# B over 128 array lines: real and imaginary part of one frequency in one output of M

## The chip, the cores and the metric

The kernel runs on one core of a Trainium2 chip. The metric is the device time of one execution in microseconds (us). The engines are called as in the profile: PE is TensorE (PEld its weight loads), ACT is ScalarE, DVE is VectorE, POOL is GpSimd, and SP only issues DMAs. Each engine works through its own instructions in the order in which the program issues them.

## The reference

Eight sequences of 3008 rows with 256 channels go through a Fourier layer and then a two-layer perceptron:

```python
X = np.fft.rfft(x, axis=1)                       # per batch, over the 3008 rows
Yr = Xr @ w_r - Xi @ w_i + b_r
Yi = Xr @ w_i + Xi @ w_r + b_i
Y  = soft_threshold(Yr, 0.01) + 1j * soft_threshold(Yi, 0.01)
y  = np.fft.irfft(Y, n=3008, axis=1)
h  = y @ w_in                                    # 256 -> 2048
g  = where(h > 0, h, exp(min(h, 0)) - 1)
out = g @ w_out                                  # 2048 -> 256
```

## The kernel before

3008 is 47 x 64, and each transform is made of two short ones. Per batch five kinds of unit follow one another:

- **A**, six units: a matmul with the 64-point matrix `M1` over 8 columns of x, copied to SBUF and stored to DRAM (`DA`).
- **X**, eight units: `Z` is read back from `DA` in another order, and eight matmuls of 96 rows against `M2` make the spectrum. A copy (`evac`, on ACT in the main part) puts it into `XT`, channels in partitions, a real plane and an imaginary plane, for 24 values of `k` times 64 values of `n2`.
- **M**, twelve units (six `q` with `i` = 0 and 1): four matmuls of 128x512. The weights of PE are 128 columns of `XT` (two `k` times 64 `n2`), the moving operand is `wcat_r` = [w_r, w_i] against the real plane and `wcat_s` = [-w_i, w_r] against the imaginary one. Output partitions are 128 frequencies, output columns are 256 real and 256 imaginary channels. DVE adds the bias (`yb`), POOL clips and subtracts, giving `Y`.
- **B**, six units: the inverse 64-point step. A frequency's real and imaginary part lie in different columns of `Y`, and each `k` owns 64 partitions, so a unit is eight matmuls over 64 partitions each, in pairs on the two halves of the array (`s` = 0, 1), two accumulated for each output. ACT copies the two PSUM banks to `Bz`, and `Bz` goes to DRAM (`DB`).
- **Y**, eight units: `Bs` is read back from `DB`, matmuls with `M4` give `yT`.

The perceptron runs in 376 iterations of 512 rows by 256 of the 2048 inner channels, 47 to a batch. An iteration has a `front` (four matmuls into `hps`, then ELU on ACT, DVE or POOL into `gT`) and the `back` of the iteration two before (eight matmuls into `ps_o`). `plan` puts at most one unit of the next batches ahead of each front, in the order X0 to X7, then M, M, B and so on, then A and Y. All units of the main part share one PSUM buffer (`psF`, one buffer), so that the copy out of a unit must be over before the next unit's first matmul. `hps` has two buffers.

The first batch has no perceptron to lie beside. It runs ahead of the loop: tables are computed on POOL, DVE and ACT (`points`, `phases`, `wraps`, `signs`, `sizes`, `sines`; group 0 to 3 of `M2`), then A, X with two PSUM buffers (copies of X1, X4 and X7 on DVE, the others on ACT), M (`first_M`, half of them with the bias added by a matmul and the clipping on ACT and DVE) and B, with short runs of idle matmuls (`idle_pe`) between. In this stretch the tables of `M3` for B are made: `v3` at L559, `w3` at L599 and L600, its absolute value at L606 after X1, two sines at L613 after X7, two multiplications at L617 and L621 beside the first M. `gate` makes POOL wait for `Z`, and behind it POOL issues the three loads of x for batch 1 and half of `w_out`, ahead of all X units.

## Time and profile before

| | |
|---|---|
| median of 3 runs | 912.52 us (912.39 to 912.84) |
| the profiled execution | 911.36 us, of which its span is 909.6 us |
| PE busy | 893.2 us, 98% of the span |
| DVE, ACT, POOL busy | 717.5, 696.8, 314.9 us |
| M (L192), matmuls 128x512 | 384, of them 48 ahead of the loop |
| B (L244), matmuls 64 rows x 256 | 384, of them 48 ahead of the loop |
| first front | 56.5 us after the span's start |

A line of the timeline or of the chain gives the start in us from the span's start, the duration, the engine, the line of the kernel and the tiles (output, arrow, inputs). Several instructions of one kind are merged ("x8"), and then the duration is from the start of the first to the end of the last. The chain of work that ended last gives only the share that nothing else covered. Matmuls overlap: a 128x512 matmul lasts 0.38 us and the next starts 0.216 us behind it.

### The profile page before, as it was taken

The numbers are of one execution on the slowest core, as the hardware profiler recorded it, in microseconds if no ns is written. First come the engines' busy times: TensorE is split into PE (matmuls) and PEld (weight loads), VectorE is DVE, ScalarE is ACT, GpSimd is POOL, SyncE is SP. The second block draws the span as 40 slices with busy tenths as digits, with TensorE's granted clock in tenths as the row PEclk, the third lists the DMA queues.
The fourth block names the chain that finished last, engine by engine and source line by source line (L and its number), as shares of the span: only waits on it lengthen the run. The fifth ranks groups of instructions, "written<-read, shape, count | busy, mean of one in ns | idle before, by whom it ended". The sixth has DMA issues, their size and how long they took to land.

```text
span 909.6 us, 17270 instructions
## 1 busy us (share of the span) xinstructions
PE 893.2 (98%) x6721; PEld 652.3 (72%) x6721; DVE 717.5 (79%) x891; ACT 696.8 (77%) x850; POOL 314.9 (35%) x438
## 2 busy tenths in 40 slices
PE   8989999999999999999999999999999999999997
PEld 3447667876688667886678766787667866777775
DVE  8669778887788778897788877888778877778776
ACT  6768788777878778787787888778887877767664
POOL 6701540333321441405404153033332134443664
PEclk9999999999999999999999999999999999999999
DMA  8997116721283215732166032752228111231011
GB/s 270 309 269 228 47 48 186 209 70 47 77 241 124 71 47 143 190 109 85 56 201 194 24 99 59 217 161 72 69 72 230 30 42 47 82 82 48 24 48 46
DMA packets 90670, 106.24 MB, mean 117 GB/s; under 512 B 5270, under 2 KB 81308, under 8 KB 87228
## 3 DMA queue, kind: packets, MB, share of 16 engines
q1 hardware_dynamic: 84332, 77.62, 30.6%
q0 software_dynamic: 5968, 27.26, 9.1%
q8 instruction: 52, 0.85, 0.4%
q10 hardware_dynamic: 288, 0.26, 0.1%
q14 instruction: 30, 0.25, 0.1%
HBM read 55.32 MB, written 49.81 MB: 116 GB/s over the span
## 4 chain that ended last, share of the span: by engine, by line
PE 85%; DVE 5%; ACT 3%; DMA 3%; issue 2%; POOL 1%; SPq 1%; DVEq 0%; ACTq 0%; POOLq 0%
PE ps_o L773 34%; PE hps L715 34%; PE mps L192 9%; PE yps L282 2%; PE bps L244 2%; PE xps L175 2%; PE aps L144 2%; DMA Bs<-DB 2%; DVE gT L742 1%; DVE Et L754 1%; ACT Et L729 1%; ACT Et L726 1%; DMA xt<-in_x_dram 1%; DVE osb L784 1%; ACT Bz L257 1%
## 5 line engine op out<-in xcount | busy, mean ns | idle before, releaser
L773 PE MATMUL ps_o<-w_out_r,gT 128*128 128x256 f32 x3008 | 477.0, 301 | 0.2 <-DVE gT L740 0.2
L773 PEld LDWEIGHTS ps_o<-w_out_r,gT 128*128 128x128 f32 x3008 | 403.4, 189 | 50.3 <-DVE osb L784 1.3
L715 PE MATMUL hps<-yT,w_in_s 128*128 128x512 bf16 (+4 forms) x1728 | 389.9, 353 | 2.5 <-DVE gT L742 1.2
L740 DVE SCALAR_TENSOR_TENSOR gT<-Et,hps 128x512 fp32r<-128x512 f32 (+1 forms) x272 | 222.8, 848 | 75.3 <-POOL Et L752 38.2
L742 DVE SCALAR_TENSOR_TENSOR gT<-hps,Et 128x1024 fp32r<-128x1024 f32 x198 | 242.2, 1223 | 16.5 <-PE ps_o L773 1.0
L715 PEld LDWEIGHTS <-w_in_s 128*128 128x128 bf16 x1728 | 141.6, 98 | 129.4 <-issue 23.0
L729 ACT ACTIVATE Et<-hps 128x1024 f32<-128x1024 f32 x198 | 204.0, 1030 | 13.2 <-PE hps L715 6.7
L752 POOL TENSOR_SCALAR Et<-Et 128x512 f32<-128x512 f32 x187 | 111.4, 615 | 222.9 <-ACT Et L724 222.9
L754 DVE TENSOR_SCALAR Et<-Et 128x1024 f32<-128x1024 f32 x198 | 137.0, 692 | 48.0 <-ACT Et L729 40.1
L210 POOL TENSOR_SCALAR clip<-yb 128x512 f32<-128x512 f32 x84 | 51.7, 615 | 316.0 <-DVE yb L202 278.6
L724 ACT ACTIVATE Et<-hps 128x512 f32<-128x512 f32 x188 | 102.1, 595 | 63.9 <-PE hps L715 63.9
L726 ACT ACTIVATE Et<-hps 128x1024 f32<-128x1024 f32 x84 | 86.3, 1027 | 71.5 <-PE hps L715 71.0
L211 POOL TENSOR_TENSOR Y<-yb,clip 128x512 bf16<-128x512 f32 x84 | 107.2, 1276 | 7.0
L727 ACT ACTIVATE Et<-Et 128x1024 f32<-128x1024 f32 x84 | 88.8, 1058 | 2.7
L202 DVE TENSOR_TENSOR yb<-mps,bias_bc 128x512 f32<-128x512 f32 x89 | 61.4, 689 | 35.4 <-PE mps L192 28.6
L127 ACT CAST XT<-xps 128x768 bf16<-128x768 f32 x61 | 48.8, 800 | 15.8 <-PE xps L175 15.8
L127 ACT CAST yT<-yps 128x752 bf16<-128x752 f32 x63 | 49.7, 788 | 14.2 <-PE yps L282 14.1
L192 PE MATMUL mps<-wcat_r,XT 128*128 128x512 bf16 x192 | 58.2, 384 | 0.8 <-ACT Bz L257 0.3
L127 ACT CAST A<-aps 128x1024 bf16<-128x1024 f32 x45 | 45.6, 1014 | 15.3 <-PE aps L144 13.8
L192 PE MATMUL mps<-wcat_s,XT 128*128 128x512 bf16 x192 | 57.1, 379 | 0.0
L192 PEld LDWEIGHTS <-XT 128*128 128x128 bf16 x384 | 30.8, 98 | 29.6 <-DVE XT L125 0.6
L257 ACT CAST Bz<-bps 128x1024 bf16<-128x1024 f32 x46 | 46.0, 1000 | 2.5 <-PE bps L244 2.5
(110 smaller groups left out, 412.9 us busy)
## 6 DMA issues: line engine op xcount, KB each, us to landing
xt<-in_x_dram POOLq DMA_DIRECT2D x21, 1024.0 KB, 7.1
out_dram<-osb SPq DMA_DIRECT2D x158, 128.0 KB
Bs<-DB SPq DMA_DIRECT2D x32, 384.0 KB
DA<-A SPq DMA_DIRECT2D x21, 512.0 KB
DB<-Bz SPq DMA_DIRECT2D x21, 512.0 KB
Z<-DA SPq DMA_DIRECT2D x7, 1152.0 KB
Z<-DA SPq DMA_DIRECT2D x11, 384.0 KB
xt<-in_x_dram POOLq DMA_DIRECT2D x6, 512.0 KB, 5.9
```

What stands on the lines that cost most here:

```text
L127: nc.scalar.copy(dst, src)
L192: nc.tensor.matmul(ps, lhsT=XT[:, dt, c, o : o + P], rhs=wm[:, dt, :], start=(not biased and m == 0 and dt == 0), stop=(m == 1 and dt == 1),)
L211: nc.gpsimd.tensor_tensor(Y_of[b, q][:, i, :], yb, clip[:], ALU.subtract)
L715: nc.tensor.matmul(hps[:, s, c0:c1], lhsT=w_in_s[:, dt, ft * P : ft * P + P], rhs=yT_of[b][:, dt, t0 : t0 + c1 - c0], start=(dt == 0), sto ...
L724: nc.scalar.activation(E_[:, s], hps[:, s], AF.Exp)
L726: nc.scalar.activation(E_, hps[:], AF.Relu, scale=-1.0)
L729: nc.scalar.activation(E_, hps[:], AF.Exp)
L740: nc.vector.scalar_tensor_tensor(o, e, -1.0, h, ALU.add, ALU.max)
L742: nc.vector.scalar_tensor_tensor(o, h, 0.0, e, ALU.max, ALU.add)
L752: eng.tensor_scalar(E_[:, s], E_[:, s], 1.0, 0.0, ALU.min, ALU.max)
L754: nc.vector.tensor_scalar(E_, E_, 1.0, -1.0, ALU.min, ALU.add)
L773: nc.tensor.matmul(po[q][:, i_ % 2, :], lhsT=gT[:, s, i_ * P : i_ * P + P], rhs=w_out_r[:, ft, :], start=(ft == 0 and i_ % 2 == 0), stop=( ...
```

## The change

- `XT` has for each `k` three runs of 64: minus imaginary, real, imaginary. `M2`'s columns are put in that order, ACT (or DVE) copies real and imaginary part, and a new POOL instruction behind each copy writes minus imaginary (128 x 384 elements), 64 in all.
- An M group takes one `k` at a time. Its weights are the 128 columns [real, imaginary] against w_r and [minus imaginary, real] against w_i, so that real and imaginary part of one frequency are 128 output partitions and 256 columns hold the channels. That is eight matmuls of 128x256 in place of four of 128x512. `wcat_s` goes, and the bias becomes a column of 128 values by 256.
- A B unit is four matmuls over all 128 partitions, none accumulated, in place of eight over 64. The two PSUM banks hold `i` = 0 and 1. Where the copy is split between ACT and DVE, each takes one bank.
- `M3` has real and imaginary rows in its two halves of partitions. It is built in two helper tiles `T3` and put in place by four DMAs from SP. The work for `T3` (`v3`, `w3`, its absolute value, two sines) moves ahead of `wraps(3)`, that is ahead of half of `M2`'s sines; the two multiplications move behind X1's copy, and the pieces of the bias from behind X1 to behind X4.
- POOL's loads of x for batch 1 move from ahead of X to behind X1, X3 and X7, and that of `w_out` to behind the first M.

```diff
             k = 8 * g + kk
             nc.tensor.matmul(
                 psv[:, kk, 0 : 4 * K1], lhsT=Z[:, k, dt * P : dt * P + P],
-                rhs=M2[:, k].rearrange("p c m -> p (c m)"), start=True, stop=True,
-            )
-        xv = XT[:, dt].rearrange("p c (m s) -> p c m s", s=NS)[:, :, :, 8 * g : 8 * g + 8]
-        pv = psv[:, :, 0 : 4 * K1].rearrange("p k (c m) -> p c m k", c=2)
-        evac(xv, pv, on_dve)
+                rhs=M2[:, k].rearrange("p k c t -> p (k c t)"), start=True, stop=True,
+            )
+        xv = XT[:, dt].rearrange("p k (a s) -> p k a s", s=NS)[:, :, :, 8 * g : 8 * g + 8]
+        pv = psv[:, :, 0 : 4 * K1].rearrange("p j (k a) -> p k a j", a=4)
+        evac(xv[:, :, 2:6], pv, on_dve)
+        nc.gpsimd.tensor_scalar(xv[:, :, 0:2], xv[:, :, 4:6], -1.0, None, ALU.mult)
...
     def m_group(b, q, i, ps, biased=False):
         XT = XT_of[b]
-        o = (2 * q + i) * P
-        if biased:
-            nc.tensor.matmul(ps, lhsT=busy[:, 0:P], rhs=bias_p[:], start=True, stop=False)
-        for m, (c, wm) in enumerate(((0, wcat_r), (1, wcat_s))):
-            for dt in range(2):
+        for e in range(2):
+            k, pe = 4 * q + 2 * i + e, ps[:, e * D : e * D + D]
+            if biased:
                 nc.tensor.matmul(
-                    ps, lhsT=XT[:, dt, c, o : o + P], rhs=wm[:, dt, :],
-                    start=(not biased and m == 0 and dt == 0), stop=(m == 1 and dt == 1),
+                    pe, lhsT=bias_p[:, D : D + P], rhs=bias_p[:, 0:D], start=True, stop=False
                 )
+            for c in range(2):
+                for dt in range(2):
+                    nc.tensor.matmul(
+                        pe, lhsT=XT[:, dt, k, (1 - c) * N2 : (1 - c) * N2 + P],
+                        rhs=wcat_r[:, dt, c * D : c * D + D],
+                        start=(not biased and c == 0 and dt == 0), stop=(c == 1 and dt == 1),
+                    )
...
-            nc.vector.tensor_tensor(yb, ps, bias_bc[:], ALU.add)
+            nc.vector.tensor_tensor(
+                yb.rearrange("p (e d) -> p e d", e=2), ps.rearrange("p (e d) -> p e d", e=2),
+                bias_bc[:].unsqueeze(1).to_broadcast([P, 2, D]), ALU.add,
+            )
...
-        for pp in range(2):
-            for c in range(2):
-                for s in range(2):
-                    nc.tensor.matmul(
-                        ps[:, s, pp * D : pp * D + D],
-                        lhsT=M3[s * N2 : s * N2 + N2, 2 * v + pp, c, :],
-                        rhs=Y[s * N2 : s * N2 + N2, pp, c * D : c * D + D],
-                        start=(c == 0), stop=(c == 1),
-                    )
+        for i in range(2):
+            for e in range(2):
+                nc.tensor.matmul(
+                    ps[:, i, e * D : e * D + D], lhsT=M3[:, e, 2 * v + i, :],
+                    rhs=Y[:, i, e * D : e * D + D], start=True, stop=True,
+                )
         o = 4 * (v % 2)
-        Bv = Bz[:, o : o + 4, :].rearrange("p (q s) d -> p s q d", s=2)
-        psv = ps[:].rearrange("p s (q d) -> p s q d", d=D)
+        Bv = Bz[:, o : o + 4, :].rearrange("p (i e) d -> p i (e d)", i=2)
         if on_dve:
-            nc.scalar.copy(Bv[:, :, 0], psv[:, :, 0])
-            nc.vector.tensor_copy(Bv[:, :, 1], psv[:, :, 1])
+            nc.scalar.copy(Bv[:, 0], ps[:, 0])
+            nc.vector.tensor_copy(Bv[:, 1], ps[:, 1])
         else:
-            nc.scalar.copy(Bv, psv)
+            nc.scalar.copy(Bv, ps[:])
...
-        pool.tensor_scalar(wcat_s[:, :, 0:D], w_i_f[:], -1.0, None, ALU.mult)
-        pool.tensor_copy(wcat_s[:, :, D : 2 * D], w_r_f[:])
         for g in range(4):
...
+            pool.tensor_scalar(
+                bias_p[:, D + N2 * c : D + N2 * c + N2], busy[:, 0:N2], (c0, c1)[c][:], None,
+                ALU.mult,
             )
...
         sines(1, 1)
+        slot0()
+        full = [P, NV, N2]
+        dve.scalar_tensor_tensor(
+            v3[:], n2row.unsqueeze(1).to_broadcast(full), 1.0 / S,
+            k3[:].unsqueeze(2).to_broadcast(full), ALU.mult, ALU.mult,
+        )
+        dve.tensor_scalar(w3[:], v3[:], CMAGIC, -CMAGIC, ALU.add, ALU.add)
+        dve.tensor_tensor(w3[:], v3[:], w3[:], ALU.subtract)
+        nc.scalar.activation(a3[:], w3[:], AF.Abs)
+        T3 = [wk4.tile([P, NV, P], BF16, name="T3", tag="Bs") for _ in range(2)]
+        for o, src, sc, bi in ((1, w3, TURN, 0.0), (0, a3, -TURN, hpi[:])):
+            nc.scalar.activation(
+                T3[0][:, :, o * N2 : o * N2 + N2], src[:], AF.Sin, bias=bi, scale=sc
+            )
         wraps(3)
         signs(2)
-        slot0()
         sines(2, 0)
         sizes(3)
         sines(2, 1)
...
     load_w_in(0)
-    gate(Z_of[0][:, 8, 0:1])
-    for ci in range(3):
-        load_x(1, ci)
-    load_w_out(0)
...
         unit_X(0, u, alone=True, on_dve=u in (1, 4, 7))
         if u == 1:
-            nc.scalar.activation(a3[:], w3[:], AF.Abs)
-            nc.vector.tensor_copy(bias_p[32:64], rest[32:64])
-            nc.vector.tensor_copy(bias_p[64:P], rest[64:P])
-            nc.vector.tensor_tensor(rest[64:P], rest[64:P], bias_p[64:P], ALU.subtract)
-            nc.vector.tensor_copy(bias_p[64:P], rest[64:P])
+            for o in range(2):
+                nc.vector.scalar_tensor_tensor(
+                    T3[1][:, :, o * N2 : o * N2 + N2], T3[0][:, :, (1 - o) * N2 : (2 - o) * N2],
+                    2.0 - 4.0 * o, sgb, ALU.mult, ALU.mult,
+                )
+            for c in range(2):
+                for e in range(2):
+                    nc.sync.dma_start(
+                        M3[N2 * c : N2 * c + N2, e], T3[c][N2 * e : N2 * e + N2]
+                    )
+        if u == 4:
+            nc.vector.tensor_copy(bp[32:64], rest[32:64])
+            nc.vector.tensor_copy(bp[64:P], rest[64:P])
+            nc.vector.tensor_tensor(rest[64:P], rest[64:P], bp[64:P], ALU.subtract)
+            nc.vector.tensor_copy(bp[64:P], rest[64:P])
+        if u == 1:
+            gate(Z_of[0][:, 8, 0:1])
+            load_x(1, 0)
+        if u in (3, 7):
+            load_x(1, (u - 1) // 2 - u // 7)
         idle_pe(1)
-    for o, src, sc, bi in ((1, w3, TURN, 0.0), (0, a3, -TURN, hpi[:])):
-        nc.scalar.activation(
-            M3[:, :, 0, o * N2 : o * N2 + N2], src[:], AF.Sin, bias=bi, scale=sc
-        )
-    sgb = sg3[:].unsqueeze(2).to_broadcast([P, K1 // 2, N2])
-    nc.vector.scalar_tensor_tensor(
-        M3[:, :, 1, 0:N2], M3[:, :, 0, N2:P], 2.0, sgb, ALU.mult, ALU.mult
-    )
     first_M(0, 0, False)
-    nc.vector.scalar_tensor_tensor(
-        M3[:, :, 1, N2:P], M3[:, :, 0, 0:N2], -2.0, sgb, ALU.mult, ALU.mult
-    )
+    load_w_out(0)
```

## The prediction

> **What bounds the kernel now.** I read the page's shares and chain first, then the chain around one B unit, then the timeline there engine by engine, then the opening (the first 57 us), and last the busy time and clock by stretch.
>
> ```profile
> PE 893.2 (98%) x6721; PEld 652.3 (72%) x6721; DVE 717.5 (79%) x891; ACT 696.8 (77%) x850; POOL 314.9 (35%) x438
> ```
>
> PE is the bound nearly everywhere, so a change on PE counts in full where nothing else is late next. The chain of work around unit B0 of batch 1 (start, duration):
>
> ```profile
> 99.25 0.86 PE hps L715 x4
> 100.11 0.92 PE ps_o L773 x8
> 101.03 0.54 PE bps L244 x8
> 101.57 0.97 PE hps L715 x4
> 102.54 0.92 PE ps_o L773 x8
> ```
>
> Only PE stands in it. B costs 0.54, and the front behind it 0.97 where its neighbour costs 0.86: 0.65 us in all. But in the timeline ACT is close behind:
>
> ```profile
> 100.15 1.03 ACT L726 ACTIVATE Et<-hps 128x1024 f32<-128x1024 f32 x1
> 101.20 1.06 ACT L727 ACTIVATE Et<-Et 128x1024 f32<-128x1024 f32 x1
> 102.17 0.99 ACT L257 CAST Bz<-bps 128x1024 bf16<-128x1024 f32 x1
> 103.31 0.39 PE L192 MATMUL mps<-wcat_r,XT 128*128 128x512 bf16 x1
> ```
>
> Three ACT instructions run back to back from the front of the M iteration, and the copy of B (ends 103.16) frees the one PSUM buffer 0.15 before the next M starts.
>
> The opening matters because it runs once with nothing beside it. Its lines, columns as before, idle time before in brackets:
>
> ```profile
> 23.81 0.80 ACT L127 CAST XT<-xps 128x768 bf16<-128x768 f32 x1 [2.10 <-PE xps L175]
> 24.61 0.94 DVE L125 CAST XT<-xps 128x768 bf16<-128x768 f32 x1
> ...
> 31.97 0.95 DVE L621 SCALAR_TENSOR_TENSOR M<-M,sg 128x768 bf16<-128x768 bf16 x1
> 32.15 1.24 POOL L230 TENSOR_SCALAR clip<-yb 128x512 f32<-128x512 f32 x1 [3.16 <-DVE yb L202]
> ...
> 46.85 0.59 ACT L254 CAST A<-bps 128x512 bf16<-128x512 f32 x1 [0.31 <-PE bps L244]
> 47.47 0.69 DVE L255 CAST A<-bps 128x512 bf16<-128x512 f32 x1 [1.10 <-ACT A L254]
> ```
>
> ACT has 2.1 us to spare before X0's copy, and none after. POOL's clip takes 1.24 beside DVE's L621, 0.61 elsewhere. B5's two half copies run one after the other. And by stretch (PE busy, PEld, DVE, ACT, POOL, clock):
>
> ```profile
> 23.30:30.50 7.20, 5.71 (x74) 3.53 (x74) 6.24 (x10) 5.46 (x8) 5.49 (x7) 1.00 0.93 251
> 30.50:46.80 16.30, 16.30 (x106) 6.99 (x106) 9.79 (x14) 11.68 (x16) 10.83 (x12) 1.00 1.03 326
> 54.00:57.40 3.40, 1.74 (x20) 1.03 (x20) 1.26 (x2) 0.79 (x1) 0.00 (x0) 1.00 1.04 318
> 57.40:60.90 3.50, 3.50 (x23) 2.04 (x21) 1.61 (x2) 2.14 (x3) 1.47 (x2) 0.51 1.03 271
> ```
>
> From 30.5 to 46.8 PE never pauses; after 3.4 us in which PE was half busy, the clock was 0.51 for the next 3.4.
>
> **The change, part by part.**
>
> *B, in the loop.* Four matmuls of 128x256 replace eight on half arrays. Full-array bf16 matmuls of that width exist:
>
> ```profile
> 485.46 1.05 PE L715 MATMUL hps<-yT,w_in_s 128*128 128x256 bf16 x8
> ```
>
> Eight last 1.05 with 0.27 for the last one, so 0.11 each, with a weight load under every one. A B unit becomes 4 x 0.11 = 0.44 and saves 0.21; 42 units in the loop could give 8.8. Next late is ACT's copy. Where PE does wait for it (copy over at 214.19, next unit at 214.24) the gap is 0.05. I read the gap for B0 to B3 of the seven batches: 24 of 28 show 0.14 to 0.19, four show 0.05. Gap less 0.05, summed, is 2.7. Behind B5 the front comes 0.10 after gT of two iterations before, which hangs on the same ACT row; so B4 and B5 together give 0.05 in six batches and some 0.3 in the last, where no A unit follows: 0.6. Total -3.3. The new copy runs through its banks in order, as A's does (1014 ns for 128x1024 at L127, against 1000 at L257): 28 x 0.014 = +0.4.
>
> *M.* 8 x 0.109 to 0.111 replaces 4 x 0.216: 0 to 0.02 more for each of 96 groups; start by start the steps of such rows are 0.109 and 0.216, so I take 0.005: +0.5 (bounds 0 and +1.9). DVE's addition (689 ns) keeps its elements.
>
> *Negation in the loop, 56 of them.* The nearest rows are the clip, 615 ns for 512 elements, so 0.46 for 384, and a cast of 128x512 to bf16 at 604; I take 0.50, with 0.46 and 1.24 as ends. In the X iterations POOL is idle, and ACT's copy of X7 ends at 89.38 with M's first matmul at 90.18. The negation ends by 89.95, and the first matmul to read it is M's third, at 90.4: cost 0, and if it took 1.24, some 0.3 in each of seven batches, +2. ACT's copy has the same 768 elements, and ACT rows go by elements (752 in 788 ns, 768 in 800): 0.
>
> *The opening: tables.* On DVE v3 (0.95), w3 (0.85 and 1.25) and slot0 (0.66) now stand ahead of wraps(3), so w3 is there at 18.1 + 3.7 = 21.8, where ACT waits for it from 18.7. Behind it on ACT: absolute value 0.85, sines 0.85 and 0.92, then five table instructions at some 0.45 and the bias copy at 0.3. X0's copy starts at 26.5, 2.7 late; the 2.1 us of cover is gone. DVE: X1's copy 27.0 to 27.95, the two multiplications (0.95 each) to 29.85, X4's copy to 30.8, the bias pieces (halved, 1.2) to 32.0, X7's copy to 32.95, against 30.44 before: +2.5.
>
> *The opening: POOL's queue.* Eight negations, the gate (0.4) and two loads (0.65 each) pass through POOL ahead of M. The negation of X1 meets the two multiplications, and by the row at 32.15 it gets through only behind them, at about 30.3. Then gate, load, two negations, load and four more: 0.4 + 1.3 + 6 x 0.5 = 4.7, so X7's is done at 35.0, and M's matmuls on minus imaginary wait for it. The second M group starts at 35.6 instead of 31.15: +4.5 (bounds: +2.5 if POOL keeps pace, +7 with negations of 0.9). The third load and that of w_out stand behind; B1 needs POOL's second Y some 6.4 us after that start and gets it at 5.9. The x loads have until A at 46.75, now some 50: 0. wcat_s no longer costs POOL 2.20 and 0.60, and two one-column products (nearest row 536 ns) come in; POOL was done with it at 25.59, ahead of the first negation: 0. SP gets four DMAs for M3, two of which wait for the multiplications; nothing is queued behind them before B0's store, and B0 is 8 us away: 0 (a store of 256 KB, DB<-A, lands in 2.8).
>
> *The opening: clock.* PE has 3 us without work behind X1 and another 2 before M. By the rows at 54.0 and 57.4 a stretch half empty is followed by 3.4 us at 0.51, in which M loses up to 1.7, over two stretches 3.4; the X stretch before, 5.71 busy of 7.20, kept 1.00. Between 0 and 3.4 I take the middle: +1.7. The Trainium skill ("TensorE: Matmul & The Clock Gate", Part 1: The HAM clock gate) lets the clock fall only after an idle window of about 3.4 us; by that rule the term would be 0 and the sum 0.65. The trace does not agree: the window ahead of the 0.51 held 1.74 us of matmuls.
>
> *The opening: B.* B0 to B3 lie on PE: 4 x 0.21 = -0.8. B4 and B5 wait for the last Y instead (45.68 + 0.69, and B5's second half behind it): 0. B5's two half copies each read half of both banks, and DVE began 0.02 after ACT ended; at 79.33 and 79.41 DVE and ACT copy two tiles of ps_o at once. With a bank each, DVE starts 0.62 earlier: -0.65 (bounds -0.65 and 0).
>
> **Sum.** -3.3 + 0.4 + 0.5 + 0 + 4.5 + 1.7 - 0.8 - 0.65 = +2.35 us. The profiled execution took 911.36 us (span 909.6), 1.16 below the median of 912.52; the sum makes it 913.7, and 912.52 + 2.3 = **914.8** on the median's scale. A difference of 0.2%, 1.8 us, is about what a measurement of this kernel can tell from none.
>
> **The rivals.**
>
> 1. *The opening absorbs the tables (not slower).* If POOL keeps pace with the copies, M starts 2.5 late and the clock stays at 1.00. For it: POOL has less to do in this stretch without wcat_s, and 23.3 to 30.5 kept its clock. Against it: the row of 1.24. The sum is zero where M's delay and the clock's term together are 3.85. Here it is 2.35 - 2.0 - 1.7 = -1.35, so 911.2; a little more of B's saving brings it below 910.7.
> 2. *B's saving arrives whole (faster).* If the copy is not late, the loop gives -8.8 in place of -2.9, and the sum is -3.6: 908.9. Against it stand the three ACT rows; it needs Bz to start 0.1 earlier, and nothing in the change makes L726 or L727 shorter.
> 3. *Negations are slow.* At 1.1 us the opening loses another 6 x 0.6 = 3.6, and in the loop a negation that starts at 89.43 ends at 90.53, past the start of DVE's next SBUF-to-SBUF instruction (L754, 90.51), which could be held as the clip was by L621. The front two iterations on has 0.10 to spare for that, and each 0.02 past it costs 56 x 0.02 = 1.1. Sum about +7: 919.5.
> 4. *The change doesn't shorten B.* If the step stayed at 0.65, the loop and the opening gain nothing: 2.35 + 2.9 + 0.8 = +6, so 918.5. The 0.11 rows speak against it.
>
> **How the numbers follow.** Forecast 0.48 (own range 913.2 to 917: two thirds, 0.32, slower by over 1.8, the rest, 0.16, within); rival 1 0.21 (0.14 within, 0.07 faster); rival 2 0.13 (faster); rivals 3 and 4 0.13 and 0.05 (slower). Faster 0.20, within 0.30, slower 0.50. The range leaves out most of rival 2 and the far half of rival 3: **909.8 to 919.5**.
>
> **What would show it.** X0's copy on ACT near 26.5; POOL without a pause from X1's negation to X7's; the second M group near 35.6; a clock below 1.00 between 27 and 41; B5's halves side by side. In the loop: B and the front behind it in 0.44 + 0.86, the next unit 0.05 behind the copy, M at 0.88, X7's negation over before M starts. The forecast is wrong if M starts by 33.5, if PE's gaps behind Bz stay at 0.15 with B shorter, or if negations last 0.8 or more.

## The result, and the profile after

The changed kernel takes **923.97 us** (median of 4 runs, 922.86 to 924.65) against 912.52 before. The ratio is 1.0119, 95% interval 1.0103 to 1.0135. The sign of the forecast held; its size did not: 914.8 was forecast, and the time lies 4.5 us above the range. The profiled execution took 922.86 us (span 920.8), 11.50 more than that of before.

The page of the changed kernel, the shares of the engines:

```profile
PE 889.6 (97%) x6818; PEld 698.7 (76%) x6920; DVE 717.1 (78%) x891; ACT 695.7 (76%) x850; POOL 386.9 (42%) x502
```

PE has 3.6 us less to do than before, and the kernel is 11.5 longer: PE waits more. POOL has 72 us more, nearly all of it in one group. The groups of POOL by form (line, engine, operation, tiles, shapes, count, then busy time, mean ns of one, idle time before):

```profile
L181 POOL TENSOR_SCALAR XT<-XT 128x384 bf16<-128x384 bf16 x64 | 75.9, 1193 | 96.6 <-ACT XT L126 96.6
L217 POOL TENSOR_SCALAR clip<-yb 128x512 f32<-128x512 f32 x84 | 51.7, 615 | 156.7 <-DVE yb L206 156.5
```

A negation takes 1.19 us, not 0.50, though it has three quarters of the clip's elements (L217). What that does to the opening is in the chain of work between 26 and 41 us (start, duration, what):

```profile
26.82 0.70 ACT XT L126
...
28.74 0.95 POOL XT L181
...
30.85 2.37 POOL XT L181 x2
33.22 0.57 POOL xt L115
33.79 0.80 POOL XT L181
34.59 0.34 issue
34.93 3.48 POOL XT L181 x3
38.41 0.05 issue
38.46 1.25 PE mps L195 x5
39.70 0.21 PE mps L190
```

From X0's copy until M, the chain is POOL's queue. X0's copy comes near its forecast (26.73 for 26.5). X7's copy ends at 34.51, 1.6 later than the 32.95 of the forecast, but its negation is over only at 38.4, and the second M group (its first matmul is L190's) starts at 39.50 in the timeline; the chain counts it from 39.70. In the kernel before, X7's copy and the start of the second M group were these lines:

```profile
29.48 0.96 DVE L125 CAST XT<-xps 128x768 bf16<-128x768 f32 x1 [0.76 <-PE xps L175]
31.15 0.38 PE L189 MATMUL mps<-bias_p,busy 128*128 128x512 bf16 x1
```

In the loop the same instruction stands at each batch's step from X to M. The timeline at batch 1's first M group:

```profile
100.32 1.16 POOL L181 TENSOR_SCALAR XT<-XT 128x384 bf16<-128x384 bf16 x1 [0.30 <-ACT XT L126]
101.02 1.24 PE L195 MATMUL mps<-wcat_r,XT 128*128 128x256 bf16 x8
101.53 0.44 PEld L195 LDWEIGHTS <-XT 128*128 128x128 bf16 x5 [0.29 <-POOL XT L181]
```

The group lasts 1.24 where the others last 1.05, because a weight load waits 0.29 for the negation. It is the fourth of the eight: X7 writes the second half of the channels, and the third load, on the first half, needs only X6's negation.

B did become shorter. The chain around B0 of batch 1, and ACT in the timeline beside it:

```profile
112.09 0.45 PE bps L250 x4
112.54 0.21 PE hps L730
112.76 0.05 issue
112.81 0.59 PE hps L730 x2
113.41 0.94 PE ps_o L788 x8
114.34 0.96 PE mps L195 x8
```

```profile
112.26 1.06 ACT L742 ACTIVATE Et<-Et 128x1024 f32<-128x1024 f32 x1
113.23 0.99 ACT L260 CAST Bz<-bps 128x1024 bf16<-128x1024 f32 x1
114.27 1.03 PE L195 MATMUL mps<-wcat_r,XT 128*128 128x256 bf16 x8
```

B and the front behind it take 0.45 + 0.85 (0.54 + 0.97 before). The copy of Bz ends at 114.22 and the next unit starts at 114.27, 0.05 behind it: ACT is next late, as forecast. So it is in 27 of the 28 units B0 to B3 of the seven batches (0.21 in the other).

The windows by stretch (PE busy, PEld, DVE, ACT, POOL, then granted clock, DMA share, GB/s) show the clock:

```profile
25.60:29.05 3.45, 1.31 (x20) 0.97 (x21) 2.53 (x5) 2.86 (x7) 1.45 (x2) 1.00 0.71 173
29.05:32.45 3.40, 2.94 (x27) 2.12 (x26) 3.32 (x5) 1.35 (x2) 3.38 (x5) 0.50 0.87 225
32.45:35.85 3.40, 2.09 (x12) 0.89 (x10) 1.84 (x3) 0.80 (x1) 3.40 (x4) 0.50 1.16 320
35.85:39.30 3.45, 1.24 (x6) 0.69 (x7) 0.00 (x0) 0.00 (x0) 3.13 (x4) 0.50 1.13 355
39.30:42.70 3.40, 3.40 (x17) 2.34 (x16) 0.69 (x1) 0.82 (x2) 2.08 (x3) 0.50 0.95 313
```

The half clock lasts from 29.05 to 42.70, four times as long as any in the kernel before, and the first stretch of M runs in it.

B5's two half copies, now with a bank each, still run one behind the other:

```profile
56.29 0.58 ACT L257 CAST A<-bps 128x512 bf16<-128x512 f32 x1 [0.29 <-PE bps L250]
...
56.91 0.69 DVE L258 CAST A<-bps 128x512 bf16<-128x512 f32 x1 [1.09 <-ACT A L257]
```

From the starts of gT, iteration by iteration against the kernel before: +10.11 at the first, +11.04 at the eleventh, +9.86 where the last batch's Y is due, +11.03 at the end. So the opening lost the time, the loop gave back 1.2, and the last batch lost another 1.2, 0.9 of it where Y waits for Bs.

### The profile page after: what moved, and what is told of

Read it like the earlier page. It is cut to its first block, busy times and chain, and to the rows that moved or that the text cites. A ratio compares the mean times of both kernels' runs of the same rounds, so it can differ in the third digit from the quotient of the medians.

```text
span 920.8 us, 17634 instructions
## 1 busy us (share of the span) xinstructions
PE 889.6 (97%) x6818; PEld 698.7 (76%) x6920; DVE 717.1 (78%) x891; ACT 695.7 (76%) x850; POOL 386.9 (42%) x502
## 4 chain that ended last, share of the span: by engine, by line
PE 82%; DVE 5%; ACT 4%; DMA 3%; issue 3%; POOL 2%; SPq 1%; DVEq 0%; ACTq 0%; POOLq 0%
PE ps_o L788 33%; PE hps L730 32%; PE mps L195 9%; PE yps L285 2%; PE aps L143 2%; PE bps L250 2%; DMA Bs<-DB 2%; PE xps L174 2%; DVE gT L757 1%; DVE Et L769 1%; POOL XT L181 1%; ACT Et L744 1%; ACT Et L741 1%; DMA xt<-in_x_dram 1%; ACT Bz L260 1%
## 5 line engine op out<-in xcount | busy, mean ns | idle before, releaser
L730 PE MATMUL hps<-yT,w_in_s 128*128 128x512 bf16 (+7 forms) x1629 | 382.4, 351 | 9.0 <-DVE gT L757 2.3
L730 PEld LDWEIGHTS <-w_in_s 128*128 128x128 bf16 x1728 | 145.4, 98 | 106.5 <-issue 16.8
L217 POOL TENSOR_SCALAR clip<-yb 128x512 f32<-128x512 f32 x84 | 51.7, 615 | 156.7 <-DVE yb L206 156.5
L181 POOL TENSOR_SCALAR XT<-XT 128x384 bf16<-128x384 bf16 x64 | 75.9, 1193 | 96.6 <-ACT XT L126 96.6
L195 PE MATMUL mps<-wcat_r,XT 128*128 128x256 bf16 x768 | 104.3, 277 | 4.1 <-POOL XT L181 3.3
L195 PEld LDWEIGHTS <-XT 128*128 128x128 bf16 x768 | 69.5, 99 | 18.4 <-POOL XT L181 5.9
```

The source lines that it names most:

```text
L195: nc.tensor.matmul(pe, lhsT=XT[:, dt, k, (1 - c) * N2 : (1 - c) * N2 + P], rhs=wcat_r[:, dt, c * D : c * D + D], start=(not biased and c = ...
L730: nc.tensor.matmul(hps[:, s, c0:c1], lhsT=w_in_s[:, dt, ft * P : ft * P + P], rhs=yT_of[b][:, dt, t0 : t0 + c1 - c0], start=(dt == 0), sto ...
```

## The experiments

Edits are against the changed kernel where nothing else is said. Ratios are against the kernel before on the same chip.

**Negations of the opening on DVE.**

```diff
-        nc.gpsimd.tensor_scalar(xv[:, :, 0:2], ...
+        (nc.vector if alone else nc.gpsimd).tensor_scalar(xv[:, :, 0:2], ...
```

> Changed kernel, but in the opening (batch 0) the eight negations run on DVE in place of POOL; the loop is as changed. Theory POOL: M waits for POOL's queue of 1.19 us negations, so the second M group moves from 39.5 us to about 35.5 (then DVE's own queue is the limit), the clock returns earlier, and the total falls by 4 to 6 us to 918-920. Rival tables: the order of tables and copies on ACT and DVE sets the start of M by itself; then the second M group stays within 1 us of 39.5 and the total within 1.5 us of 924.

Measured: 925.21 us, ratio 1.0143 (1.0128 to 1.0158), no gain at all, so neither theory as written. A negation takes 0.25 to 0.39 on DVE, and the second M group starts at 36.73, 2.8 earlier. B0 starts at 41.87 (45.0 in the changed kernel), the first gT 2.0 earlier. But between the third and the seventh gT it loses 3.7 against the kernel before, more than all that. The chain of this kernel there:

```profile
63.93 13.66 DMA DA<-A
...
77.71 1.24 DVE gT L759
```

The fourth gT waits 2.31 us for a store of batch 1's A that is 13.66 us in the DMA queues, because a tile of A lies in a buffer of gT. That is most of the loss; the rest, up to the seventh gT, was not followed.

**Tables of M3 in their old place.** `v3`, `w3`, absolute value, sines and multiplications as in the kernel before, the four transfers of M3 behind the first M group; negations on POOL as changed.

> Changed kernel with the tables of M3 back where they were before (w3 ahead of X, its absolute value and the bias pieces behind X1, sines and multiplications behind X7; the four DMAs follow them); the negations stay on POOL. X0's copy goes back from 26.7 to about 23.9. Theory POOL: the queue of eight negations, gate and two loads, 11 us, starts some 3 us earlier and its end with it: second M group near 36.3, total 920 to 921; M3's DMAs land late and may cost up to 2 of that. Rival tables: with them gone M starts as before at 31 to 32, total 914 to 916.

Measured: 923.2, ratio 1.0129 (1.0098 to 1.0160). X0's copy is back at 23.53 and X7's ends at 30.15, but the negations run until 35.6 and the second M group starts at 36.69, as theory POOL had it: POOL alone holds it. The first gT is 7.5 behind the kernel before, and then again 3.6 are lost up to the seventh, so that the time is not the 920 to 921 of that theory.

**Both.**

> Both: negations of the opening on DVE and tables back in their old place. Every theory has the second M group within 1.5 us of the old 31.15 here; the loop's own difference is left: the trace of the changed kernel gives +0.9 us from the first to the last gT, so the total should be 913 to 915 if M3's late DMAs cost nothing, up to 917 if B0 waits for them.

Measured: 923.34, ratio 1.0119 (1.0104 to 1.0135). The second M group starts at 32.15, only 1.0 behind the kernel before, and yet the kernel is not faster. In the timeline:

```profile
43.30 0.37 PE L252 MATMUL bps<-Y,M 128*128 128x256 bf16 x1 [7.05 <-DMA M<-T]
```

B0 waits 7.05 us for M3's transfers. Issued here from 31.7 on, not from 27.0 as in the changed kernel, they share the DMA engines with 4 MB of x and `w_out`.

**More idle matmuls behind the X units.**

```diff
-        idle_pe(1)
+        idle_pe((1, 12, 2, 2, 2, 3, 2, 18)[u])
```

> Changed kernel with more idle matmuls between the X units of the opening (12 behind X1, 18 behind X7, 2 or 3 elsewhere), so that PE is not empty while it waits. Theory clock: the clock stays at 1.00 where it was 0.5 from 29 to 43 us; M's first 4 us run at full speed and the total falls by 1.5 to 2.5 us. Rival: the half clock lies beside POOL's waits and costs nothing; total within 0.7 us of 924.

Measured: 919.63, ratio 1.0082 (1.0067 to 1.0097): 4.3 less than the changed kernel. The windows of this kernel over the same stretches:

```profile
25.60:29.05 3.45, 2.87 (x26) 1.65 (x26) 2.53 (x5) 2.86 (x7) 1.39 (x2) 1.00 0.77 178
29.05:32.45 3.40, 3.28 (x41) 2.14 (x41) 3.32 (x6) 2.23 (x3) 3.38 (x5) 1.00 0.85 224
```

With PE busy for 2.87 of 3.45 the clock stays at 1.00; with 1.31 it fell. The second M group comes only 0.4 earlier (39.07), since POOL holds it; M and B then run at full clock, and the first gT comes 1.9 earlier, near the 1.7 forecast for the clock. The profiled executions differ by 3.3: another 0.1 up to the last batch's Y, and 1.3 in the last batch, which loses nothing here (+7.83 to +7.72); Y there waits 1.00 for Bs and not 1.99. Why that went with it was not tried.

**The copy of B split between ACT and DVE in the loop.**

```diff
-        if on_dve:
+        if on_dve or not alone:
```

> The changed kernel (923.97), with the copy of B split in the loop as B5's was ahead of it: bank 0 on ACT, bank 1 on DVE. Theory 1: in the loop B is 0.10 us shorter on PE and nearly all of it is lost again because ACT's copy (0.99 us, behind two other ACT instructions) frees the one PSUM buffer late. Then the gap from the end of PE's work on the iteration to the next unit's first matmul opens from 0.05 to 0.14 or more, and the loop's 42 units give 2 to 4 us: 920 to 922. Rival: DVE, which must then find another 0.6 us 42 times, is late with its own instruction (gT) and PE waits for that: 924 to 928, with waits of PE's weight loads for DVE in the iterations that hold B. The two half copies each read one bank alone; if one bank was what kept B5's halves apart before, they run side by side here, otherwise DVE begins only where ACT ends.

Measured: 952.36, ratio 1.0438 (1.0424 to 1.0452): the rival, and far beyond its 924 to 928. The timeline at B0 of batch 1:

```profile
121.12 0.61 PE L250 MATMUL bps<-Y,M 128*128 128x256 bf16 x4
122.42 0.57 ACT L257 CAST Bz<-bps 128x512 bf16<-128x512 f32 x1
123.02 0.69 DVE L258 CAST Bz<-bps 128x512 bf16<-128x512 f32 x1 [1.60 <-ACT Bz L257]
123.76 1.03 PE L195 MATMUL mps<-wcat_r,XT 128*128 128x256 bf16 x8 [0.22 <-DVE Bz L258]
```

DVE starts when ACT has ended, each with its own bank. Together they take 1.29 us where ACT's one copy takes 0.99, so the buffer comes free later, and DVE's next gT is late too: 28.4 us over 42 units, 0.68 each. What orders the two is a wait for ACT's half, not a bank that they share; whether the program or the chip puts it there stays open.

**Prices on POOL.** The kernel before, with negations and a memset that nothing reads, near 60 us.

```diff
+ nc.gpsimd.tensor_scalar(v[:, 0:384], v[:, 1536:1920], -1.0, None, ALU.mult)          # bf16, one run
+ nc.gpsimd.tensor_scalar(r[:, :, 0:2, 0:8], r[:, :, 2:4, 0:8], -1.0, None, ALU.mult)  # bf16, runs of 8
+ nc.gpsimd.memset(y2[:], 1.0)
+ nc.gpsimd.tensor_scalar(yt[:, 0:384], y2[:, 0:384], -1.0, None, ALU.mult)            # f32, one run
```

> The kernel before, with extra work on POOL near 60 us that nothing reads (three times: a negation of 128x384 bf16 in one run, one of 128x384 bf16 in runs of eight elements as the new plane has them, a memset, and one of 128x384 f32 in one run). Theory 1 (the element size or the type makes it slow): the first two take 1.1 to 1.2 us alike, the third about 0.46. Theory 2 (the short runs make it slow): only the second takes 1.2, the first and third about 0.46. Theory 3 (it costs that only next to DVE): all vary from 0.46 to 1.2 with what DVE does beside them.

Measured: 1.17 to 1.69 us, 1.16 to 1.57 and 1.17 to 1.60. Neither type nor runs make it slow; none of the theories had the f32 one as slow as the rest. So the clip was the wrong row for a reason that all three share.

**M3 ahead of the loads.** Negations on DVE and the tables in their old place, and POOL issues the loads of x and `w_out` one by one behind M groups, when M3 has landed.

> The kernel with negations on DVE and the tables of M3 in their old place (923.34), in which B0 still started at 43.3 us although M's second group was back at 32.2. Here the three loads of x and the load of w_out, which were ahead of M3's four transfers or beside them, are issued by POOL only when M3 has landed, between M's groups. Theory 1: M3's transfers are short by themselves (2 to 3 us) and B0 waits because they share the DMA engines with 4 MB of loads. Then M3 is there by 37, B0 starts at 36 to 38 in place of 43.3, the first gT comes at 60 to 63 in place of 70, and the kernel takes 914 to 917. Rival: the transfers take 8 us or more whatever runs beside them, since they go from SBUF to SBUF; then B0 stays at 42 to 44 and the time at 922 to 924. Second rival: the loads, now late, hold A or the stores of B instead; then B0 is early but the first gT comes at 66 or later.

Measured: 924.47, ratio 1.0132 (1.0118 to 1.0145). B0 starts at 36.45, as theory 1 had it: M3's transfers are short when nothing runs beside them. But the second rival holds as well:

```profile
64.53 1.43 PE L287 MATMUL yps<-M,Bs 96*128 96x94 bf16 x16 [8.81 <-DMA Bs<-DB]
```

The loads, issued 13 to 18 us later than in the kernel before, hold the last stores of B, and Y waits 8.81 us for Bs (1.01 in the kernel before). In the stretch from 26 to 62 us the loads, M3's 0.8 MB, which are new, and B's stores delay one another.

**M with [real, imaginary] first.**

```diff
-        for e in range(2):
-            for c in range(2):
+        for c in range(2):
+            for e in range(2):
```

> The changed kernel (923.97), in which an M group does the four matmuls on [real, imaginary] first and the four on [minus imaginary, real] after them; before, the third of the eight already needed the new plane. Theory 1: at each batch's step from X to M the group waits 0.3 us for X7's negation, which now ends 1.17 us behind the copy; two more matmuls ahead of it hide 0.22. Then the first M group of a batch lasts 0.95 to 1.05 in place of 1.24, the seven batches give 1.5 to 2, and the kernel takes 922 to 922.5. Rival: the wait moves to the ACT or DVE instruction that is next, and the time stays within 0.5 of 923.97. If it grows, the new order of accumulation costs PE something by itself.

Measured: 922.10, ratio 1.0101 (1.0086 to 1.0116), 1.9 less than the changed kernel, though the two intervals overlap. A batch's first M group lasts 1.05 like all others in six of seven batches (1.23 to 1.41 in the changed kernel), as theory 1 had it. In the profiled execution, the slowest of the five (924.33), the loop gives back 2.0 up to the last batch's Y where the changed kernel gives back 1.2, so that 0.8 of the 1.9 is seen in a trace.

**The form of POOL's instruction.** The kernel before, with forms that nothing reads.

```diff
+ nc.gpsimd.tensor_scalar(fd, fs, -1.0, None, ALU.mult)               # L681
+ nc.gpsimd.tensor_scalar(fd, fs, -1.0, 0.0, ALU.mult, ALU.add)       # L682
+ nc.gpsimd.tensor_scalar(fd, fs, LAM, -LAM, ALU.min, ALU.max)        # L683
+ nc.gpsimd.tensor_scalar(dst, src, -1.0, 0.0, ALU.mult, ALU.add)     # L684
+ nc.gpsimd.tensor_scalar(dst, src, LAM, -LAM, ALU.min, ALU.max)      # L685
```

> The kernel before with other extra work on POOL near 60 us that nothing reads, three times over. In the run with priced negations neither the type nor the runs of eight made a difference (1.16 to 1.6 us for 128x384, all of them), while the clip (128x512, minimum and maximum) takes 0.61. Theory 1 (the form counts: an instruction with one operation takes longer than one with two): of the f32 ones in one run, the negation with one operation takes 1.2, the negation with an addition of zero behind it 0.46, minimum and maximum 0.46; in bf16 runs of eight the negation with an addition of zero takes about 0.5. Theory 2 (multiplication counts): both negations take 1.2, minimum and maximum 0.46. Theory 3 (neither counts, and POOL is slow there because of its neighbours or right behind a load): all take about 1.2. The subtraction of two tensors and the copy, in the same runs of eight, tell whether another way of making the plane would be cheaper than 1.19.

Measured (first and third of the three rounds):

```profile
62.59 1.18 POOL L681 TENSOR_SCALAR pf<-pf 128x384 f32<-128x384 f32 x1
63.85 0.51 POOL L682 TENSOR_SCALAR pf<-pf 128x384 f32<-128x384 f32 x1
64.45 0.51 POOL L683 TENSOR_SCALAR pf<-pf 128x384 f32<-128x384 f32 x1
64.92 0.95 POOL L684 TENSOR_SCALAR XT<-XT 128x384 bf16<-128x384 bf16 x1
...
75.16 1.41 POOL L681 TENSOR_SCALAR pf<-pf 128x384 f32<-128x384 f32 x1
76.65 0.51 POOL L682 TENSOR_SCALAR pf<-pf 128x384 f32<-128x384 f32 x1
...
77.72 0.51 POOL L684 TENSOR_SCALAR XT<-XT 128x384 bf16<-128x384 bf16 x1
78.31 0.51 POOL L685 TENSOR_SCALAR XT<-XT 128x384 bf16<-128x384 bf16 x1
```

Theory 1: with one operation 1.18 to 1.49, with a second behind it 0.51. Two of the three at L684 took 0.95, the third 0.51 like the one beside it with minimum and maximum. The two slow ones lie beside an instruction of DVE from SBUF to SBUF (Et<-Et, 64.58 to 65.50 and 70.85 to 71.83), as the slow clip of the prediction did; beside the third DVE is idle. A subtraction of two tensors takes 0.83, a copy 0.50 to 0.85.

**The changed kernel with that form.**

```diff
-        nc.gpsimd.tensor_scalar(xv[:, :, 0:2], xv[:, :, 4:6], -1.0, None, ALU.mult)
+        nc.gpsimd.tensor_scalar(xv[:, :, 0:2], xv[:, :, 4:6], -1.0, 0.0, ALU.mult, ALU.add)
```

> The changed kernel (923.97) with one thing different: the negation adds zero behind the multiplication, the form that took 0.51 us for 128x384 where the form with one operation took 1.2 to 1.5. Theory 1 (the price of the negation was the term that failed): the negations last 0.51 in the loop and 0.5 to 0.95 in the opening, X7's is over at 35 to 35.8 in place of 38.4, the second M group starts at 35.4 to 36.2 in place of 39.5, and the first gT comes 3 to 4 earlier; the 0.3 per batch ahead of M goes too (2.0 in all). The time is then 917 to 919.5. If the rest of the forecast held as well it would be 914.8. Rival (other limits lie right behind POOL's, as when DVE made the negations): the second M group starts at 36 to 37 but the gain of the opening is under 1.5, so 920.5 to 922 with the loop's part.

Measured: 917.98 (915.78 to 918.88), ratio 1.0055 (1.0044 to 1.0067): theory 1, and 6.0 less from one operand. The negations in the loop last 0.52 on average. The timeline at X7's copy and the start of M:

```profile
32.99 0.96 DVE L124 CAST XT<-xps 128x768 bf16<-128x768 f32 x1
34.03 0.51 POOL L181 TENSOR_SCALAR XT<-XT 128x384 bf16<-128x384 bf16 x1 [0.21 <-DVE XT L124]
34.60 0.72 PE L195 MATMUL mps<-wcat_r,XT 128*128 128x256 bf16 x5 [0.20 <-POOL XT L181]
35.16 0.27 PE L190 MATMUL mps<-bias_p 128*128 128x256 bf16 x1
```

The second M group starts at 35.16; 35.6 had been forecast. But POOL now waits for X7's copy, not M for POOL's queue. The first gT is 4.05 behind the kernel before, the ninth 5.15, and the loop gives back 2.8 up to the last batch's Y (2.4 forecast). Then 3.5 are lost at once:

```profile
802.22 0.56 PE L285 MATMUL yps<-M,Bs 96*128 96x94 bf16 x8 [3.04 <-DMA Bs<-DB]
```

In the last batch Y waits 3.04 us for Bs (1.03 in the kernel before, 1.99 in the changed one), and half clock follows for 3.4 us.

**That, with M's order and idle matmuls** (12 behind X1, 10 behind X7, 2 or 3 behind the others).

> The changed kernel with three of the edits at once: negations with a second operation, the M group with [real, imaginary] first, and idle matmuls behind the X units of the opening (12 behind X1, 10 behind X7, 2 or 3 behind the others). By themselves the idle matmuls gave 4.3 and the order in M 1.9. Theory 1 (they act on different waits): no half clock ahead of 60, the second M group at 35.2 to 35.8, the first gT at 65 to 66.5, each batch's step from X to M without a wait, and 913 to 916 in all. Rival (the opening is held by M3's transfers and the loads as soon as POOL is not): the second M group comes at 35.5 but B0 stays at 41 or later, and the time is 916.5 to 919.

Measured: 916.81, ratio 1.0041 (1.0028 to 1.0054). The clock stays at 1.00 until 63, and yet the time is the rival's, by another way: X7's copy comes at 34.87 (32.99 without), since two of DVE's pieces of the bias took 1.45 and 1.06 where they had taken 0.32 and 0.50, and the second M group starts at 36.82. POOL's negations run beside these pieces in both traces, so why they are slow here stays open.

**Two loads early, two late**: as with M3 ahead of the loads, but two of x as in the kernel before, and the two-operation form.

> The kernel in which M3's transfers came first (924.47) and the loads behind them held the stores of B, with two differences: the negation has its second operation (on DVE in the opening, on POOL in the loop), and two of the three loads of x are issued where the kernel before had them, ahead of the X units, so that 2 MB are through before M3's transfers begin at 31; the third load and that of w_out come behind M3 as there. Theory 1 (the opening is a budget of DMA time: 4 MB of loads, M3's 0.8 MB and B's stores must all be through before Bs is read): B0 starts at 36 to 38.5, B's last stores are issued by 50.5 without a pause, the first gT comes at 61 to 64, and with the loop 2.5 shorter the time is 911 to 914.5. Rival (M3's transfers wait for the two early loads too, as they did with all four): B0 at 40 or later, first gT at 65 or more, and 916 to 919.

Measured: 919.98, ratio 1.0088 (1.0075 to 1.0102), slower than even the rival had it. B0 starts at 38.54, near theory 1, after 2.63 of waiting for M3. But B1 comes only at 42.63, behind POOL's gate on M3, Y waits 3.27 for Bs, and the first gT is 8.4 behind the kernel before.

**The last store of B on ACT's queue**, with the two-operation form.

```diff
-            nc.sync.dma_start(DB_of[b][k0 : k0 + 8].rearrange("k p d -> p k d"), Bz[:])
+            (nc.scalar if (b, v) == (7, 5) else nc.sync).dma_start(...)
```

> The changed kernel with the two-operation negation (917.98), and the last batch's last store of B issued by ACT behind its own copy, not by SP behind five stores of the output. In the trace without that, the iterations up to the last batch's Y were 2.35 behind the kernel before, then PE waited 3.0 us for Bs (1.0 in the kernel before), half clock followed for 3.4 us, and the kernel ended 5.9 behind. Theory 1 (the queue of SP costs the last 3.5): Y waits for under 0.5, no half clock near 800 us, and the time is 914.3 to 915.6, beside the 914.8 of the forecast. Rival (Bs is late because the transfers themselves are slow): Y still waits for 2 or more and the time stays at 917.5 to 918.5.

Measured: 917.12 (915.75 to 917.98), ratio 1.0044 (1.0029 to 1.0059). Y no longer waits, there is no half clock near 800, and the last batch gains 1.2 where the one above lost 3.5. But the median fell by 0.9 only, which the intervals can't tell from nothing: in this profile the opening, which is the same program, is worse (second M group at 36.56, two stretches of half clock, and a store of A that is 13.16 us in the DMA queues ahead of the fourth gT), 8.28 behind at the ninth gT.

**The opening rearranged**: in addition `v3` and `w3` behind M2's tables, ACT's absolute value and sines between X's copies, the loads one by one behind M groups.

> The same with the tables of M3 rearranged: on DVE v3 and w3 behind the tables of M2, on ACT the absolute value and the two sines between the copies of X0 to X3, the two multiplications behind X4's copy, and POOL's loads of x and w_out one by one behind the first M groups, when M3 has landed. Theory 1 (the opening lost its time to the place of the tables): X0's copy at 23.8 to 24.5 in place of 26.5, the second M group at 32 to 33.5 in place of 35.2, B0 at 36 to 37.5, the first gT at 61 to 62.5, and 911 to 913. Rival (the loads, 5 us later than before, hold the last stores of B again): B0 as above, but Y's first matmul at 59 or later, first gT at 64 or more, and 914.5 to 917.

Measured: 917.73, ratio 1.0049 (1.0035 to 1.0063): the rival, 0.7 beyond its range. The second M group at 32.32 and B0 at 36.25 are what theory 1 asked for, 1.2 and 1.1 behind the kernel before, and Y then waits 5.70 for Bs.

**The sum**: two operations, the last store on ACT, idle matmuls.

> The changed kernel with the two-operation negation, the last store of B on ACT, and idle matmuls behind the X units of the opening (12 behind X1, 8 behind X7, 2 or 3 behind the others). With the first two alone two openings of the same program came out 3 us apart at the eighth gT (5.2 and 8.3 behind the kernel before), with one or two stretches of half clock ahead of M. Theory 1 (that spread is the clock's): at full clock throughout, the first gT comes at 64 to 65, the eighth iteration is 5 to 5.5 behind, the loop gives back 2.8 and the last batch 1: 913.8 to 915. Rival (the transfers behind the opening, not the clock, set the eighth gT): it is 6.5 or more behind, and the time is 915.5 to 917.

Measured: 915.80 (915.44 to 917.29), ratio 1.0043 (1.0029 to 1.0056): the rival, and by the ratio no better than the last store alone (1.0044) or the three edits at once (1.0041). Full clock until 62, and yet the ninth gT is 7.75 behind, so the clock alone does not set it. X7's copy comes at 34.38, behind slow pieces of the bias as above, and the second M group at 36.55. The first gT comes at 66.31, later than theory 1 had it; loop and last batch give back 2.9 together, where it expected 3.8.

**The last store on ACT's queue, in the kernel before.**

> The kernel before, in which the last batch's last store of B is issued by ACT behind its copy in place of SP behind five stores of the output. In its trace Y of the last batch waits 1.0 us for Bs. Theory 1: that wait goes and the kernel takes 911.3 to 912. Rival: the next unit or DVE is as late as Bs, and nothing changes (912.3 to 912.9).

Measured: 912.46 against 912.19, ratio 1.0000 (0.9992 to 1.0009). In its trace the last batch gains 1.2 as well, but the first iterations lose 1.4; in the median nothing is left. So the last batch's wait is in the kernel before too, and taking it away can't be told from nothing here.

## Why the prediction was wrong

The sum was +2.35; the profiled executions differ by 11.50. By stretches, from the starts of the second M group, B5's end (46.82 before, 56.25 after, 50.73 with two operations) and the gT's:

| | forecast | changed kernel | with two operations |
|---|---|---|---|
| second M group | +4.5 | +8.35 | +4.01 |
| from there to B5's end | +0.9 | +1.08 | -0.10 |
| from there to the first gT | -0.65 | +0.68 | +0.14 |
| first gT to the ninth or eleventh | 0 | +0.93 | +1.10 |
| loop up to the last batch's Y | -2.4 | -1.18 | -2.80 |
| the rest | 0 | +1.64 | +3.95 |
| sum | +2.35 | +11.50 | +6.30 |

- **"A cast of 128x512 to bf16 at 604; I take 0.50, with 0.46 and 1.24 as ends."** This is the step that failed: the price of a negation, 0.50 taken and 1.19 measured. The 1.19 lay within the ends, and at that price rival 3 is the case that came. One operand decides it: with a second operation the price in the loop is 0.52, and 6.0 of the 9.2 us by which the forecast was missed are gone. The 3.2 that are left lie mostly in the wait for Bs in the last batch. The trace of before had a row of this very form, a multiplication by minus one with no second operation, which I quoted only as work that goes away:

```profile
L522 POOL TENSOR_SCALAR wcat_s<-w_i_f 128x512 bf16<-128x512 f32 x1 | 2.2, 2201 | 0.0
```

  2.20 for 512 elements scale to 1.65 for 384 (DVE worked beside it, which may be part of it). Going by the same engine and operation name and not by the whole form, I took the clip, which has two operations. The Trainium skill ("GPSIMD Engine Reference", section 3.1) gives about 1.8 cycles an element at 1.2 GHz as the best case of a simple loop, from which 0.58 us is an estimate for 384 elements. The runs took 0.51 with two operations, a little less than that best case, and 1.19 with one, twice as much.
- **Rival 3 named the place, not the size.** It had 3.6 for the opening and 7 in all, 919.5. The one operand measured 6.0 in the median and 5.2 between the profiled executions: 4.3 at the second M group, 1.7 more up to the first gT, 1.6 in the loop, less 0.2 in the first iterations and 2.3 at the end, where the two-operation version met the longer wait for Bs. In the loop the place was the one that the part on the negations gave (M's first group, "some 0.3 in each of seven batches, +2"; the matmul that waits is M's fourth, not its third), not the DVE instruction of rival 3.
- **The second M group, +4.5.** The 4.01 with two operations is close, but partly by luck: two errors offset each other. X7's copy ended 3.5 behind the kernel before, not 2.5, as the bias pieces took 1.95 and not 1.2. POOL added 0.5 behind it, not 2.0: X1's negation was over at 29.13, beside the second of the two multiplications, and not at 30.3 behind both. In the three other profiles with the same tables and the same negation the group came at 36.55 to 36.82.
- **The transfers of M3 at 0, and the loads at 0.** In the place that the change gives them, M3's transfers held B0 by nothing, as it was late anyway, and by 0.22 with two operations. But I looked for what is queued behind the issues on SP and POOL, and not at the DMA engines, and they are next when the work is moved: B0 waited 7.05 for M3, or Y 8.81 for Bs, or a gT 2.31 for a store of A. The opening has several limits close together (POOL's negations, the tables on ACT and DVE, DMA, clock), so the four edits that moved negations, tables or loads to another engine or place, with one operation in the negation, changed the time by only -0.8 to +1.2 us.
- **Clock, +1.7.** Right in size for the changed kernel: 1.9 up to the first gT by the run with idle matmuls. The half clock lasted 13.65 us and not two times 3.4, but most of it lay beside the wait for POOL, and M lost in its last 3.4. With the negation at the price that I had taken, the half clock (27.70 to 31.15) was over before M in that profile; in another of the same opening a second stretch (34.75 to 38.25) met M. So the term depends on how busy PE is in each stretch, and stays uncertain. The Trainium skill ("TensorE: Matmul & The Clock Gate", Part 1: The HAM clock gate) lets the clock fall after an idle window of about 3.4 us. The trace disagrees again: the window ahead held 1.31 us of matmuls.
- **B5's halves, -0.65.** Wrong: the bank was not what kept them apart.
- **B, -3.3 with ACT's copy next late, and M, +0.5.** Right: the gap behind Bz's copy is 0.05, and the loop up to the last batch gains 2.8 where the negation doesn't hold it. M with the change costs 0.010 more a group (0.884 against 0.874 from its first matmul to the front's), 0.8 in the loop, within the bounds. That rules out rivals 2 and 4. What B saves on PE is not in its matmuls, though: the two halves of the array already worked at the same time (each pair starts 3 ns apart, the pairs 106 to 117), so eight half matmuls took no longer than four full ones. From the last matmul ahead of the unit to the first behind it the time fell from 0.75 to 0.56, and nearly all of these 0.19 are at the unit's two ends.
- **Tables, X0's copy at 26.5.** Right (26.73) on ACT; on DVE X7's copy ended 1.6 later than I had it, and 1.0 later with two operations. Rival 1 is out: even where POOL kept pace, M started 4.0 late and not 2.5.
- **The last batch.** Not in the forecast. The wait for Bs behind SP's stores of the output grew from 1.03 to 1.99. Why it varies so between versions is not settled, nor why two kernels with the same opening end it 3 us apart.

## What to carry to other kernels

Price a new instruction by a row of the same engine with the same number of operations and operands, and look for that row among the work that the change removes. Ahead of a loop, where several engines and the DMA engines end within a few us of each other, sum the bytes as well as the instructions: the four transfers of M3 cost 0.2 us where their issue began 12 us ahead of their use, and 7 us where it began 5 us ahead, beside 4 MB of loads. When one run of an edit lands on the forecast, look at each step on the way there, and at other runs of the same code, before calling the step right. And a saving on the bound engine is worth what the next unit's buffer allows, here about 0.09 of 0.19 us a unit.

## What the runs showed of the hardware

- POOL's `tensor_scalar` with one operation took 1.16 to 1.73 us for 128x384 whatever the type or the runs; with a second, neutral one 0.52 on average in the loop (0.50 to 0.97), and up to 1.15 in the opening beside DVE's multiplications from SBUF to SBUF.
- The clock went to half after a stretch of 3.45 us with PE busy for 1.31, stayed there over stretches of 2.94, 2.09 and 1.24, and came back after one of 3.40 in 3.40. With 2.87 in 3.45 at full clock it did not fall, and neither did it with 2.06 in 3.40 (22.20 to 25.60 in the changed kernel). Over the first 100 us of all the traces here, cut into stretches of 3.41 us that begin where the clock changes, the 27 full-clock stretches that half clock followed had PE busy for 0.00 to 1.84 us; the least busy that it did not follow had 1.80, then 1.89. At half clock the stretches that full clock followed had 3.01 or more (one had 2.68), the others at most 3.00. So in these traces the clock went with PE's busy time in a whole stretch, and at full clock the border lay at about half of it.
- Between matmuls on the full array and a unit on half arrays the step was 209 ns going in and 202 coming out; with the unit on the full array it was 118 and 109 (medians of 42 units).
- Two copies out of two banks of one PSUM tile, on ACT and DVE, ran one behind the other (0.57, then 0.69).
